# Sigmoid attention and a gated feed-forward product on one core: both dense products by Strassen's algorithm over pairs of batches, and the attention in 64x64 tiles

## The chip, the core and the metric

The kernel runs on one core of a Trainium2 chip. The metric is the device time of one execution in microseconds (us). Of the core's engines, PE (TensorE) multiplies matrices into PSUM, which the program uses as eight banks of 512 fp32 columns on 128 partitions; ACT (ScalarE) and DVE (VectorE) work elementwise and read PSUM as well as the on-chip memory SBUF; POOL (GpSimd) works elementwise and is used here on SBUF alone; SP (SyncE) issues the DMA transfers between DRAM and SBUF. Each engine takes its instructions in the order in which the program issues them to it, and a semaphore holds an instruction until what it needs is there.

## The reference

```python
scores = scale * np.matmul(q, k.transpose(0, 1, 3, 2)) - np.log(S)     # q, k, v: 8 x 12 x 448 x 64
attn = 1.0 / (1.0 + np.exp(-scores))
attn_out = np.matmul(attn, v)
x = attn_out.transpose(0, 2, 1, 3).reshape(B * S, H * D)               # 3584 x 768
h = x @ w_in                                                           # 768 x 2048
g = h * np.clip(h + 3.0, 0.0, 6.0) / 6.0
out = g @ w_out                                                        # 2048 x 768
```

There are 8 batches of 448 tokens and 12 heads of 64 columns. All inputs are float32 and reach the device as they are, the two weight matrices as 64-bit words of two floats each.

## The kernel before, in words

**Products in three passes.** Operands of the two dense products are of type float32r, for which a matmul has one record in the profile. Every such operand is cut in two, a rounded high part and the rest, and each product is high x high, high x rest and rest x high: three matmuls of 128 rows by 128 weight columns by 512 tokens. The first product (`moe_in`, line 240) does, for each of 7 token tiles of 512 and each of 16 blocks of 128 hidden columns, 6 x 3 matmuls into one PSUM bank (L250). ACT then makes relu(h + 3) and DVE multiplies (L254, L255), and the result goes to DRAM. The second product (`moe_out`, line 383) reads it back, splits it, and does 16 x 3 matmuls for each of 7 x 6 blocks of the output (L390). Both products have 2016 matmuls.

**Attention.** Work is in pairs of heads, 64 columns each, so that a pair fills 128 partitions. A head pair has 448 keys, three blocks of 128 and one of 64. A step computes the scores of one block of keys for both heads (L167: each head uses 64 of the rows of the PE array and all 128 columns), ACT makes the sigmoid (L169, 128 x 896), and a later step multiplies with v (L200: 128 rows, 64 columns for each head). The 64-key rests of two head pairs make one step together in four tiles of 64 x 64 (L165, L198). These matmuls are plain fp32, which PE takes in two passes, so that each has two records in the profile (576 for the 288 matmuls of L167). There are 7 steps for two head pairs, 21 for a batch, 168 in all. Scores are issued three steps in a row, then the products with v of the three steps before, and so on. When a head pair is done, ACT copies its rounded part out of PSUM and DVE the rest (L215, L216).

**The two weight matrices.** They come in as 64-bit words. `join_f64` and `split_f32` (lines 46 to 67) take w_in apart on ACT, DVE and POOL in 32 pieces of 128 x 384 while the attention of the first three batches and the first token tile run; DVE's five instructions stand on L51, L52, L53, L56 and L57, POOL's two on L60 and L66. `split_over` (line 69) does the same to w_out on ACT and DVE in 24 pieces of 128 x 512 (L73 to L85), beside the last token tile of `moe_in`. Each weight is prepared once and stays in SBUF.

**The order.** It is written out by hand: attention of batches 0 to 2, `moe_in` of tiles 0 and 1, then attention of one batch and `moe_in` of one tile in turn, and the whole of `moe_out` at the end. POOL has nothing to do after the w_in pieces. SP's order is not part of the hand-written one; a scheduler makes it, in both kernels.

## Time and profile before

| what | value |
|---|---|
| median of three runs | 1212.89 us (1212.23 to 1213.55) |
| profiled execution, first to last instruction | 1209.4 us |
| PE busy | 1200.7 us |
| DVE busy | 365.9 us |
| ACT busy | 372.9 us |
| POOL busy | 64.6 us |
| moved by DMA | 128.84 MB |

The profile is of one execution; its span is 3.5 us below the median of the timed runs. A row of the profile names line, engine, operation, output and inputs, the number of partitions by elements, and then busy time and mean duration of one instruction. "PEld" is the loading of weights into PE, which runs beside the matmuls. The chain of waits follows the last instruction back to what released it; a view in order of time gives start, duration, engine and line.

### The profile page before, as it was taken

How to read it: one execution, taken by the hardware profiler on the slowest of the kernel's cores; microseconds unless marked ns; L12 is line 12 of the kernel's file. 1: busy time of each engine (PE TensorE's matmuls, PEld its weight loads, DVE VectorE, ACT ScalarE, POOL GpSimd, SP SyncE). 2: the span in 40 equal slices, each digit the busy share in tenths (PEclk: the TensorE clock that was granted, in tenths of full speed). 3: DMA queues.
4: the chain of work that ended last, by engine and by line, in shares of the span. 5: the costliest groups of instructions: out<-in, count | busy, mean ns of one | idle time of the engine just before them, and what ended most of it. 6: DMA issues, size and time to landing. Idle time of an engine off the chain costs nothing.

```text
span 1209.4 us, 13744 instructions
## 1 busy us (share of the span) xinstructions
PE 1200.7 (99%) x5568; PEld 852.6 (70%) x5568; DVE 365.9 (30%) x606; ACT 372.9 (31%) x501; POOL 64.6 (5%) x70
## 2 busy tenths in 40 slices
PE   8999999999999999999999999999999999999998
PEld 3334888837855863883785588888888888888887
DVE  3556743111111111111111389871120303030300
ACT  6886321162144135116214444340110202020200
POOL 1334520000000000000000000000000000000000
PEclk9999999999999999999999999999999999999999
DMA  7666421132133114113212278632040404040000
GB/s 241 193 194 184 154 96 62 70 114 76 61 96 95 70 68 122 61 66 115 80 62 80 79 231 292 216 118 109 28 164 27 157 27 165 27 165 18 27 27 27
DMA packets 52433, 128.84 MB, mean 107 GB/s; under 512 B 9233, under 2 KB 16017, under 8 KB 48785
## 3 DMA queue, kind: packets, MB, share of 16 engines
q1 hardware_dynamic: 52080, 127.75, 31.4%
q8 instruction: 44, 0.72, 0.3%
q10 hardware_dynamic: 288, 0.20, 0.1%
q14 instruction: 21, 0.16, 0.0%
HBM read 87.56 MB, written 40.37 MB: 106 GB/s over the span
## 4 chain that ended last, share of the span: by engine, by line
PE 99%; DMA 0%; DVE 0%; ACT 0%; issue 0%
PE ph L250 38%; PE po L390 38%; PE sc L167 10%; PE pv L200 10%; PE sc L165 2%; PE pv L198 2%; DMA qk<-qk 0%; DVE x L216 0%; ACT x L215 0%; DVE o L403 0%; ACT o L406 0%
## 5 line engine op out<-in xcount | busy, mean ns | idle before, releaser
L250 PE MATMUL ph<-x,wi 128*128 128x512 f32 x2016 | 458.9, 389 | 1.3 <-DVE x L216 1.3
L250 PEld LDWEIGHTS ph<-x,wi 128*128 128x128 f32 x2016 | 378.0, 188 | 84.0 <-issue 3.5
L390 PE MATMUL po<-gh,woh 128*128 128x512 f32 x672 | 261.4, 389 | 0.0
L390 PE MATMUL po<-gl,woh 128*128 128x512 f32 x672 | 261.4, 389 | 0.0
L390 PE MATMUL po<-gh,wol 128*128 128x512 f32 x672 | 261.4, 389 | 0.0
L169 ACT ACTIVATE a<-sc,bias_s 128x896 f32<-128x896 f32 x168 | 157.4, 1008 | 51.2 <-PE sc L167 51.0
L254 ACT ACTIVATE g<-ph,bias 128x512 f32<-128x512 f32 x112 | 77.1, 688 | 294.6 <-PE ph L250 288.0
L255 DVE SCALAR_TENSOR_TENSOR g<-g,ph 128x512 f32<-128x512 f32 x112 | 76.9, 686 | 286.8 <-ACT g L254 286.8
L350 ACT CAST gh<-gr 128x2048 fp32r<-128x2048 f32 x28 | 53.6, 1914 | 296.4 <-PE po L390 294.1
L390 PEld LDWEIGHTS po<-gl,woh 128*128 128x128 f32 x672 | 126.1, 188 | 26.4
L390 PEld LDWEIGHTS po<-gh,woh 128*128 128x128 f32 x672 | 126.1, 188 | 26.1
L390 PEld LDWEIGHTS po<-gh,wol 128*128 128x128 f32 x672 | 126.1, 188 | 26.1
L167 PE MATMUL sc<-qk 64*128 64x448 f32 x576 | 127.9, 568 | 3.8 <-DMA qk<-qk 3.8
L200 PE MATMUL pv<-a,v 128*64 128x448 f32 x576 | 122.4, 550 | 0.0
L399 DVE TENSOR_SCALAR o<-po 128x512 f32<-128x512 f32 x41 | 28.3, 690 | 284.0 <-PE po L390 283.9
L167 PEld LDWEIGHTS sc<-qk 64*128 64x128 f32 x576 | 50.6, 189 | 77.3 <-issue 37.1
L200 PEld LDWEIGHTS pv<-a,v 128*64 128x64 f32 x576 | 35.6, 136 | 80.4 <-issue 77.3
L216 DVE TENSOR_TENSOR x<-pv,x 128x448 fp32r<-128x448 f32 (+6 forms) x78 | 32.7, 419 | 194.9 <-ACT x L215 194.9
L351 DVE TENSOR_TENSOR gl<-gr,gh 128x2048 fp32r<-128x2048 f32 x28 | 64.1, 2288 | 30.2 <-ACT gh L350 30.2
L215 ACT CAST x<-pv 128x448 fp32r<-128x448 f32 (+6 forms) x78 | 28.8, 370 | 37.2 <-DVE x L216 14.3
L60 POOL TENSOR_TENSOR wis<-wis 128x384 f32<-128x384 f32 x32 | 32.4, 1011 | 95.3 <-DVE wis L57 95.3
L66 POOL TENSOR_TENSOR wi<-wis,wi 128x384 fp32r<-128x384 f32 x32 | 32.5, 1024 | 7.8 <-ACT wi L65 7.6
(33 smaller groups left out, 307.7 us busy)
## 6 DMA issues: line engine op xcount, KB each, us to landing
gd<-g SPq DMA_DIRECT2D x112, 256.0 KB, 2.4
gr<-gd SPq DMA_DIRECT2D x28, 1024.0 KB, 5.5
qk<-qk SPq DMA_DIRECT2D x47, 448.0 KB, 3.4
wis<-wi SPq DMA_DIRECT2D x32, 384.0 KB, 3.3
ws<-wo SPq DMA_DIRECT2D x24, 512.0 KB, 4.7
outT<-o SPq DMA_DIRECT2D x41, 256.0 KB, 2.0
v<-vP SPq DMA_DIRECT2D x24, 224.0 KB, 2.6
v<-vP SPq DMA_DIRECT2D x24, 192.0 KB, 2.8
```

The costliest lines, as they stand in the source:

```text
L60: nc.gpsimd.tensor_tensor(out=a, in0=a, in1=b, op=ALU.add)
L66: nc.gpsimd.tensor_tensor(out=lo, in0=a, in1=hi.bitcast(F32), op=ALU.subtract)
L167: nc.tensor.matmul(sc[:, j, :S], k[halves[j], c * P : (c + 1) * P], q[halves[j]], start=True, stop=True)
L169: nc.scalar.activation(a, sc[:, :, :S], AF.Sigmoid, bias=bias_s, scale=scale)
L200: nc.tensor.matmul(out, v[:, j * NC + c], a[:, j], start=(p % 2 == 0 and c == 0), stop=(p % 2 == 1 and c == NC - 1),)
L216: nc.vector.tensor_tensor(out=xl, in0=pt[:, q0 : q0 + w], in1=xh.bitcast(F32), op=ALU.subtract)
L250: nc.tensor.matmul(ph, w[:, cc], x, start=(n == 0), stop=(n == 3 * NCC - 1))
L254: i1 = nc.scalar.activation(g, ph, AF.Relu, bias=bias_3, scale=1.0)
L255: i2 = nc.vector.scalar_tensor_tensor(out=g, in0=g, scalar=6.0, in1=ph, op0=ALU.min, op1=ALU.mult)
L350: nc.scalar.copy(gh, gr)
L351: nc.vector.tensor_tensor(out=gl, in0=gr, in1=gh.bitcast(F32), op=ALU.subtract)
L390: nc.tensor.matmul(po[t, ec], w[:, fc], x[:, u], start=(fc == 0 and n == 0), stop=(fc == NFC - 1 and n == 2))
```

## The change

**Strassen.** The tokens of two whole batches (2 x 448) are the two column halves of x; the 768 rows of x and w_in are two halves of 384, the 2048 hidden columns two halves of 1024. The first product is computed with seven products of such quarters in place of eight (in the form with 15 additions), the second likewise with w_out. One matmul now has 448 columns where it had 512, and each of the two products still has 2016 of them: 4 pairs of batches x 8 blocks x 7 products x 9 matmuls. Operands are still cut in two and take three passes.

The sums and differences that the algorithm wants are made in these places. `prep` takes one block of a weight matrix apart (five DVE instructions of 128 x 768, twice), joins it on POOL (four of 128 x 384) and makes the sums of the quarters on POOL (four more); the seven results go to DRAM, for 8 blocks of w_in and 8 of w_out. `t_ops` makes the four differences of x on POOL and cuts the seven operands in two on DVE (`put`: a cast and a subtraction). `quad` does the first product for one block: `split_w1` cuts each weight sum, read back from DRAM for every pair of batches, on ACT and DVE; seven products go to PSUM, three of them onto the bank of the first; ACT keeps two of them, DVE makes c12, h11, h22 and h12 (`add`), ACT and DVE make the gate of each (`gate`), POOL the four differences of g, and seven tiles of 128 x 448 go to DRAM. `block` does the second product with the same cuts (`split_2`), and ACT and DVE form the output.

**Attention in 64 x 64.** Scores and products with v are issued as four matmuls on the four 64 x 64 tiles of the array, for the rests as for the whole blocks. Scores of one step and the product with v of the step two before alternate one by one. Score tiles have two buffers of two banks where there were three, the products with v have four banks, and `take` adds two banks into one tile on ACT and DVE.

**The order.** Every call is put into a list with a place, a time in us that the program works out with 0.82 us for a half step of the attention (TS) and 0.2 us for a matmul of 448 columns (TM); the list is sorted by it and issued. The places set the order on each engine and nothing else. The runs are: batches 0 to 2 and the first product of pair 0; batches 3 and 4 and pair 1; 5 and 6 and pair 2; 7 and pair 3; then the second product. Five of the eight w_in blocks are prepared in the first run of attention, three beside the first quads, and the w_out blocks one every 30 us of place from the first product of pair 1 on, up to that of pair 2.

**What stands on DVE now.** First DVE in the kernel before, in the first product of tile 1, blocks 5 to 10 (g is the gated result, ph the PSUM bank):

```order
L255 SCALAR_TENSOR_TENSOR g_5_1677<-g_5_1677,ph_5_1655 128x512
L255 SCALAR_TENSOR_TENSOR g_6_1700<-g_6_1700,ph_6_1681 128x512
L255 SCALAR_TENSOR_TENSOR g_7_1723<-g_7_1723,ph_7_1704 128x512
L255 SCALAR_TENSOR_TENSOR g_8_1746<-g_8_1746,ph_8_1727 128x512
L255 SCALAR_TENSOR_TENSOR g_9_1769<-g_9_1769,ph_9_1750 128x512
L255 SCALAR_TENSOR_TENSOR g_10_1792<-g_10_1792,ph_10_1773 128x512
```

One instruction stood there for each 18 matmuls of PE. Now DVE in the first product of pair 0, block 1, beside the preparation of w_in block 6 (ab and st are its scratch tiles, w a weight sum and its parts, raw the sum read from DRAM, za and zb PSUM banks, sn the kept sums, ga the gate):

```order
L264 TENSOR_TENSOR w_1_6_1422<-raw_1_1_1216,w_1_6_1422 128x384
L264 TENSOR_TENSOR w_2_0_1438<-raw_2_0_1269,w_2_0_1438 128x384
L301 TENSOR_TENSOR sn_1_c_1456<-za_1_1381,sn_1_1_1436 128x448
L101 TENSOR_SCALAR ab_6_1_1444<-ab_6_1_1444 128x768
L102 TENSOR_SCALAR ab_6_1_1444<-ab_6_1_1444 128x768
L103 SCALAR_TENSOR_TENSOR ab_6_1_1444<-st_6_1_1312,ab_6_1_1444 128x768
L264 TENSOR_TENSOR w_2_1_1461<-raw_2_0_1269,w_2_1_1461 128x384
L111 TENSOR_SCALAR ab_6_1_1444<-ab_6_1_1444 128x768
L112 SCALAR_TENSOR_TENSOR ab_6_1_1444<-st_6_1_1312,ab_6_1_1444 128x768
L301 TENSOR_TENSOR sn_1_h_1479<-zb_1_3_1446,sn_1_0_1420 128x448
L315 SCALAR_TENSOR_TENSOR ga_1_1481<-ga_1_1481,sn_1_h_1479 128x448
L264 TENSOR_TENSOR w_2_2_1484<-raw_2_0_1269,w_2_2_1484 128x384
```

Between the two additions on L301, which read PSUM, stand six instructions that read and write SBUF alone; the gate on L315 stands directly behind the addition that it needs.

**What stands on PE now.** PE in the attention of the kernel before (sc are score tiles, a the sigmoids, pv the banks of the products with v):

```order
L200 MATMUL pv_265<-a_209,v_156 64x448 x2
L200 MATMUL pv_265<-a_214,v_156 64x448 x2
L167 MATMUL sc_286<-qk_185 128x448 x2
L167 MATMUL sc_291<-qk_185 128x448 x2
L167 MATMUL sc_296<-qk_228 128x448 x2
L200 MATMUL pv_265<-a_244,v_156 64x448 x2
L198 MATMUL pv_265<-a_251,v_156 64x448 x2
L198 MATMUL pv_307<-a_251,v_186 64x448 x2
```

And PE in the attention now:

```order
L175 MATMUL sc_1_2_254<-qk_1_130 64x448 x4
L201 MATMUL pv_1_0_264<-a_1_0_237,v_1_131 64x448
L201 MATMUL pv_1_1_265<-a_1_0_237,v_1_131 64x448
L201 MATMUL pv_1_0_264<-a_1_0_237,v_1_131 64x448
L201 MATMUL pv_1_1_265<-a_1_0_237,v_1_131 64x448
L170 MATMUL sc_1_3_276<-qk_1_130 64x448 x2
L170 MATMUL sc_1_3_276<-qk_4_164 64x448 x2
L201 MATMUL pv_1_0_264<-a_1_1_248,v_1_131 64x448
```

Every row has outputs of 64 partitions, and groups of three steps have become groups of one.

The core of the diff, old lines first:

```diff
-                xh, xl = xb[t, cc]
-                for w, x in ((wih[fc], xh), (wih[fc], xl), (wil[fc], xh)):
-                    nc.tensor.matmul(ph, w[:, cc], x, start=(n == 0), stop=(n == 3 * NCC - 1))
-                    n += 1
-                    yield
-            g = xpr.tile([P, T], F32, tag="g", name=f"g_{t}_{fc}", bufs=2)
-            i1 = nc.scalar.activation(g, ph, AF.Relu, bias=bias_3, scale=1.0)
-            i2 = nc.vector.scalar_tensor_tensor(out=g, in0=g, scalar=6.0, in1=ph, op0=ALU.min, op1=ALU.mult)
-            evac.append((i1.ins, i2.ins))
-            nc.sync.dma_start(out=gd[t][fc // GF][:, fc % GF], in_=g)
...
-            for n, (w, x) in enumerate(((woh[ec], gh), (woh[ec], gl), (wol[ec], gh))):
-                nc.tensor.matmul(
-                    po[t, ec], w[:, fc], x[:, u], start=(fc == 0 and n == 0), stop=(fc == NFC - 1 and n == 2)
-                )
...
+            nc.vector.tensor_scalar_min(a, a, F64_TOP)
+            nc.vector.tensor_scalar(out=ai, in0=ai, scalar1=3, scalar2=None, op0=ALU.logical_shift_left)
+            nc.vector.scalar_tensor_tensor(
+                out=ai, in0=high, scalar=-(2**31), in1=ai, op0=ALU.bitwise_and, op1=ALU.bitwise_or
+            )
...
+            nc.vector.tensor_scalar(out=bi, in0=ai, scalar1=-(2**23), scalar2=None, op0=ALU.bitwise_and)
+            nc.vector.scalar_tensor_tensor(
+                out=b, in0=low.bitcast(U32), scalar=2.0**-52, in1=b, op0=ALU.mult, op1=ALU.mult
+            )
...
+                nc.gpsimd.tensor_tensor(out=o, in0=a[:, hs], in1=b[:, hs], op=ALU.add)
...
+            w = wt[0]
+            for o, x, y, op in (
+                (P5, NW, P4, ALU.add), (P6, P5, P1, ALU.subtract), (P7, P1, NW, ALU.subtract), (P3, P2, P6, ALU.subtract)
+            ):
+                nc.gpsimd.tensor_tensor(out=w[:, o], in0=w[:, x], in1=w[:, y], op=op)
...
+        for u in range(2):
+            at(place + u * gap, head, u)
+            at(place + u * gap + 1.0, body, u)
+            at(place + u * gap + 1.5, tail, u)
+        at(place + 2 * gap, sums)
...
-                    nc.tensor.matmul(sc[:, j, :S], k[halves[j], c * P : (c + 1) * P], q[halves[j]], start=True, stop=True)
...
+                for h in range(2):
+                    for j in range(2):
+                        ks = slice(c * P + h * D, c * P + (h + 1) * D)
+                        nc.tensor.matmul(sc[halves[h], j, :S], k[halves[j], ks], q[halves[j]], start=True, stop=True)
...
+                    for h in range(2):
+                        shared = h == (1 - j if second else j)
+                        nc.tensor.matmul(
+                            pv[b, hp][h][halves[j], :S], v[halves[h], j * NC + c], a[halves[h], j],
+                            start=c == 0 and not (second and shared), stop=c == NC - 1 and not (shared and not second),
+                        )
...
+        nc.scalar.copy(x, p0[:, :S])
+        nc.vector.tensor_tensor(out=x, in0=p1[:, :S], in1=x, op=ALU.add)
...
+        nc.vector.tensor_copy(x[:, 0], src)
+        nc.vector.tensor_tensor(out=x[:, 1], in0=src, in1=x[:, 0].bitcast(F32), op=ALU.subtract)
...
+        at(place, diff, P5, raw(b12), raw(b11))
+        at(place + 0.01, place_of, P1, raw(b11))
+        at(place + 1.0, place_of, P2, raw(b21))
+        at(place + 1.1, diff, P6, raw(b22), of(P5))
+        at(place + 2.0, place_of, P5, of(P5))
+        at(place + 2.1, diff, P7, raw(b22), raw(b12))
+        at(place + 3.0, place_of, P3, raw(b22))
+        at(place + 3.1, diff, P4, raw(b21), of(P6))
+        at(place + 4.0, place_of, P6, of(P6))
+        at(place + 5.0, place_of, P7, of(P7))
+        at(place + 6.0, place_of, P4, of(P4))
...
+        nc.scalar.copy(w[:, 0], src)
+        nc.vector.tensor_tensor(out=w[:, 1], in0=src, in1=w[:, 0].bitcast(F32), op=ALU.subtract)
...
+                    nc.tensor.matmul(
+                        z[k][:, :S], w[:, wu, c * P : (c + 1) * P], X[n, k, c][:, xu],
+                        start=i == 0 and k in (P1, P5, P2, P3), stop=i == 3 * HC - 1, skip_group_check=True,
...
+            nc.vector.tensor_tensor(out=t, in0=z[k][:, :S], in1=sn[s], op=ALU.add)
...
+            nc.scalar.activation(g[o], h, AF.Relu, bias=bias_3, scale=1.0)
+            nc.vector.scalar_tensor_tensor(out=g[o], in0=g[o], scalar=6.0, in1=h, op0=ALU.min, op1=ALU.mult)
...
+        def diffs():
+            a, c = g["a"], g["c"]
+            nc.gpsimd.tensor_tensor(out=a[:, 1], in0=g["g12"], in1=g["g11"], op=ALU.subtract)
+            nc.gpsimd.tensor_tensor(out=a[:, 2], in0=g["g22"], in1=a[:, 1], op=ALU.subtract)
...
+        for k in range(NW):
+            at(place + k * TU, product, k)
+            at(place + (k + 1) * TU - 10.0, split_w1, n, j, k)
...
+        at(place + 1 * TU + e, keep, P1)
+        at(place + 2 * TU + e, keep, P5)
+        at(place + 3 * TU + e, add, "c12", P6, P5)
+        at(place + 4 * TU + e, add, "h11", P2, P1)
+        at(place + 4 * TU + e + 0.1, gate, "g11", lambda: sn["h11"])
+        at(place + 5 * TU + e, add, "h22", P7, P5)
+        at(place + 5 * TU + e + 0.1, gate, "g22", lambda: sn["h22"])
+        at(place + 6 * TU + e, add, "h12", P3, "c12")
+        at(place + 6 * TU + e + 0.1, gate, "g12", lambda: sn["h12"])
+        at(place + 6 * TU + e + 0.2, diffs)
+        at(place + 7 * TU + e, gate, "g21", lambda: z[P1][:, :S])
+        at(place + 7 * TU + e + 0.1, last)
...
+        split_w((n, k, u), w2[k][:, u])
...
+        nc.scalar.copy(x[:, 0], src)
+        nc.vector.tensor_tensor(out=x[:, 1], in0=src, in1=x[:, 0].bitcast(F32), op=ALU.subtract)
...
+                for i, (wu, xu) in enumerate(passes):
                     nc.tensor.matmul(
-                        out, v[:, j * NC + c], a[:, j],
-                        start=(p % 2 == 0 and c == 0), stop=(p % 2 == 1 and c == NC - 1),
+                        z[k][e][:, :S], w[:, wu, e * P : (e + 1) * P], x[:, xu],
+                        start=u == 0 and i == 0 and k in (P1, P5, P2, P3), stop=u == HF - 1 and i == 2,
+                        skip_group_check=True,
                     )
...
+    now = 5.0
+    runs = [(0, 1, 2), (3, 4), (5, 6), (7,)]
+    marks = []
+    for n, bs in enumerate(runs):
+        steps = [(b, m, r) for b in bs for m in range(HC) for r in range(LC)]
+        lag = 2
+        for i in range(len(steps) + lag):
+            if i < len(steps):
+                b, m, r = steps[i]
+                at(now, scores, b, m, r)
+                if r in (0, NC):
+                    hp = m + HC * (r == NC)
+                    at(now - 12 if (b, m) != (0, 0) else -20 + r, load_qkv, b, hp)
+                now += TS
+                at(now, sigmoid, b, m, r)
+            if i >= lag:
+                b, m, r = steps[i - lag]
+                at(now, av, b, m, r)
+                now += TS
+                if r in (NC, LC - 1):
+                    hp = m + HC * (r > NC)
+                    at(now + 0.3, take, b, hp)
+                    if b % 2 and r == LC - 1:
+                        t_ops(b // 2, m, now + 1.0)
+        if bs[-1] % 2:
+            now += 8.0
+        marks.append(now)
+        for j in range(HF):
+            quad(n, j, now)
+            now += NW * TU
+    for j in range(HF):
+        prep(0, j, (14 + 20 * j) if j < 5 else marks[0] + 12.6 * (j - 5), 5)
+        prep(1, j, marks[1] + 5 + 30 * j, 9)
```

More of the change, by code (lines that the diff above doesn't have):

```diff
@@ L187, in av @@
[L187 to L199 removed]
+                    h = j if u == 0 else 1 - j
@@ new lines, in tile_kernel, with order @@
+    for j in range(HF):
+        prep(0, j, (14 + 20 * j) if j < 5 else marks[0] + 12.6 * (j - 5), 5)
+        prep(1, j, marks[1] + 5 + 30 * j, 9)
+    att_end = marks[3] + 8
+    at(att_end, open_two)
+    at(now + 3.0, close_one)
+    first = now
+    for n in range(NT):
+        block(n, now)
+        now += NW * HF * TU
+    def order(item):
+        place, i, f, args = item
+        if f is load_w2 and args[0] >= 2:
+            place = max(place, first + 3.01)
+        return place, i
+    todo.sort(key=order)
@@ L409, in tile_kernel @@
[L409 to L414 removed]
+        for _, _, f, args in todo:
+            f(*args)
 def kernel(q, k, v, moe_w_in, moe_w_out):
```

564 lines of the change are left out of this document (257 added, 307 removed).

## The prediction

> **What bounds the kernel now.** The head of the page comes first, then the chain of waits in order of time.
>
> ```profile
> PE 1200.7 (99%) x5568; PEld 852.6 (70%) x5568; DVE 365.9 (30%) x606; ACT 372.9 (31%) x501; POOL 64.6 (5%) x70
> ```
>
> ```profile
> 0.73 3.07 DMA qk<-qk
> 3.85 4.49 PE sc L167 x12
> ...
> 21.29 2.40 PE pv L200 x12
> 23.69 2.46 PE sc L167 x12
> ...
> 112.02 130.82 PE ph L250 x576
> 242.84 2.52 PE sc L167 x12
> ...
> 278.25 65.53 PE ph L250 x288
> ...
> 748.93 456.97 PE po L390 x2016
> ```
>
> PE is busy from 3.85 us to the end and the chain stays on it, so today time is the number of matmuls times their spacing. In the first product that is 130.82/576 = 227.1 ns, in the second 456.97/2016 = 226.7 ns, for 512 columns. One batch of attention takes from 242.84 to 278.25 = 35.4 us, 21 steps. Everything else is hidden, and the list of waits gives PE one wait of any size inside the run:
>
> ```profile
> PE ph L250 <- DVE x L216: 1.3, 1, 1.3
> ```
>
> The question is therefore how much shorter PE's work becomes, and whether DVE and POOL, which get far more to do, can still hide.
>
> **The matmuls of the two products.** Their number stays 2016 each; columns go from 512 to 448. In proportion a matmul would take 198.3 ns; if nothing in it shrank, 226.7. I take 200.0, near the proportion with a small fixed part: 4032 x 0.2000 = 806.4 us in place of 457.9 + 457.0 = 914.8, that is -108.4 us (-115 to 0).
>
> **The attention.** The loads of PE's weights show the matmuls' beat, since each pair of loads goes with a pair of matmuls:
>
> ```profile
> 47.12 0.14 PEld L200 LDWEIGHTS pv<-a,v 128*64 128x64 f32 x2 [0.23 <-issue]
> 47.50 0.14 PEld L200 LDWEIGHTS pv<-a,v 128*64 128x64 f32 x2 [0.23 <-issue]
> 47.88 0.14 PEld L200 LDWEIGHTS pv<-a,v 128*64 128x64 f32 x2 [0.23 <-issue]
> ...
> 51.18 0.21 PEld L198 LDWEIGHTS pv<-a,v 64*64 64x64 f32 x8 [0.65 <-issue]
> 52.09 0.20 PEld L200 LDWEIGHTS pv<-a,v 128*64 128x64 f32 x4 [0.70 <-issue]
> ```
>
> Inside one tile shape a pass comes every 0.38 us, so a half step (two passes) takes 0.76. Four 64 x 64 tiles do the same work at once, but alone between other shapes they took 52.09 - 51.18 = 0.91: leaving a shape cost 0.15. Now all are 64 x 64 and no shape is left inside a run: 336 half steps x 0.76 = 255.4 us against 8 x 35.4 = 283.3, -27.9 us. The ends are 0.82 each (2.46/3, -7.8) and 0.91, if each half step still drained (+22). With two score buffers, PE waits some 0.4 us for the first sigmoid of each of four runs: +2.
>
> **What DVE, ACT and POOL must do.** Groups by line give mean durations, DVE's first, then ACT's, then POOL's:
>
> ```profile
> L53 DVE SCALAR_TENSOR_TENSOR wis<-wis 128x384 int32<-128x384 int32 x32 | 19.3, 602 | 1.1
> L57 DVE SCALAR_TENSOR_TENSOR wis<-wis 128x384 f32<-128x384 uint32 x32 | 17.9, 558 | 1.1
> L76 DVE SCALAR_TENSOR_TENSOR wa<-ws,wa 128x512 int32<-128x512 int32 x24 | 16.4, 684 | 0.1
> L51 DVE TENSOR_SCALAR wis<-wis 128x384 f32<-128x384 f32 x32 | 15.3, 480 | 17.3 <-ACT wis L50 16.9 <-issue 0.4
> L52 DVE TENSOR_SCALAR wis<-wis 128x384 int32<-128x384 int32 x32 | 14.3, 447 | 1.1
> L56 DVE TENSOR_SCALAR wis<-wis 128x384 int32<-128x384 int32 x32 | 11.5, 360 | 1.1
> L74 DVE TENSOR_SCALAR wa<-wa 128x512 f32<-128x512 f32 x24 | 10.1, 422 | 11.3 <-ACT wa L73 11.2
> L216 DVE TENSOR_TENSOR x<-pv,x 128x448 fp32r<-128x448 f32 x12 | 7.5, 625 | 46.5 <-ACT x L215 46.5
> L184 DVE CAST x<-pend 128x320 fp32r<-128x320 f32 x6 | 1.9, 320 | 0.0
> ```
>
> ```profile
> L50 ACT ACTIVATE wis<-wis 128x384 f32<-128x384 f32 x32 | 17.9, 560 | 0.1
> L65 ACT CAST wi<-wis 128x384 fp32r<-128x384 f32 x32 | 16.5, 515 | 25.1 <-POOL wis L60 25.1
> L73 ACT ACTIVATE wa<-ws 128x512 f32<-128x512 f32 x24 | 16.3, 678 | 50.4 <-DMA ws<-wo 40.5 <-DVE wol L85 4.7 <-DVE g L255 2.8
> L215 ACT CAST x<-pv 128x448 fp32r<-128x448 f32 x12 | 6.4, 534 | 5.5 <-PE pv L200 3.0 <-PE pv L198 2.4
> ```
>
> ```profile
> L60 POOL TENSOR_TENSOR wis<-wis 128x384 f32<-128x384 f32 x32 | 32.4, 1011 | 95.3 <-DVE wis L57 95.3
> ```
>
> Scaled to their new widths: two tensors of 384 elements 0.56, of 448 0.62, of 768 0.94 (0.56 + 3 x 0.126); one tensor with scalars of 768 0.55; the cast of 448 0.38; an addition from PSUM 0.625; POOL 1.01 and, for 448, 1.18. A quad (7 products, 12.6 us of PE) then asks DVE for 7 x 0.56 + 4 x 0.625 + 4 x 0.62 = 8.9 us. Three of its gates stand directly behind the addition whose relu ACT must first make (0.62 plus the hand-over, 0.7), so DVE waits 2.1 more: 11.0. A `prep` costs DVE 2 x (3 x 0.55 + 2 x 0.94) = 7.06 and POOL 8 instructions; a quad gives POOL 4. ACT has 7 x 0.515 + 2 x 0.534 + 4 x 0.62 = 7.2 of 12.6 and stays behind DVE. In the second product a unit of 1.8 us asks ACT for about 1.1 and DVE for 1.2, split eight units ahead, and POOL is idle: hidden.
>
> **DVE beside POOL.** DVE in order of time, then POOL, at a place where both work:
>
> ```profile
> 115.59 1.05 DVE L52 TENSOR_SCALAR wis<-wis 128x384 int32<-128x384 int32 x1
> 116.68 1.26 DVE L53 SCALAR_TENSOR_TENSOR wis<-wis 128x384 int32<-128x384 int32 x1
> 117.97 0.36 DVE L56 TENSOR_SCALAR wis<-wis 128x384 int32<-128x384 int32 x1
> ```
>
> ```profile
> 115.37 1.06 POOL L60 TENSOR_TENSOR wis<-wis 128x384 f32<-128x384 f32 x1 [5.44 <-DVE wis L57]
> 116.39 1.13 POOL L66 TENSOR_TENSOR wi<-wis,wi 128x384 fp32r<-128x384 f32 x1
> ```
>
> A DVE instruction that meets a POOL one takes 0.70 us longer (1.05 against 0.36, 1.26 against 0.56) and ends 0.2 to 0.4 after it: they don't share, one waits. How often they met is in the means: L51, L52 and L53 lie 0.12, 0.09 and 0.04 over the undisturbed 0.36 and 0.56, 0.25 us for two POOL instructions, 0.125 each or 18% of the 0.70, with DVE about half busy. Beside a nearly full DVE they meet more often; I take the middle between 0.125 and meeting two times in three (0.47).
>
> [...]
>
> **What that adds to PE's time.** PE depends on DVE closely in a quad: the addition after product P6 must be done before P7, one product (1.8 us) later, and that of P7 before P4.
> - 23 quads without `prep`: 11.0 + 4 x 0.125 = 11.5 at best, 13.4 with three meetings of 0.8, against 12.6: +0.3 each, 7 us (0 to 18).
> - 3 quads of pair 0 with a w_in `prep` each: 11.0 + 7.06 + 12 x 0.125 = 19.6 to 23.9 (8 meetings of 0.72): +7.0 to +11.3 each; 27 us (21 to 34).
> - Of the eight w_out `prep`s, 18 us long and 30 apart by their places, 5.5 fall into quads: 7.06 + 1.0 to 3.8, less 1.6 of spare time: +6.5 to +9.2 each; I take 7.5, 41 us (36 to 51).
> - Attention of batch 1: three blocks of 7 x 1.52 = 32 us bring DVE 21 `put`s of 1.0, two `prep`s and 6 x 0.625 = 38.9 us, and POOL 28 instructions (3.5 to 13 us of DVE's time). `take` stands behind them on DVE, and PE needs its banks again after about 3 us: +12 (7 to 17). Batch 5, with one `prep` in its last two blocks: +4 (1 to 7). Batches 3 and 7 fit.
> - Before the last quads PE waits for `take`, `put` and POOL's differences of the last heads: P1's part is there 0.53 + 0.625 + 1.0 = 2.2 us after the attention, P6's at 6.2 to 9.8 where two products cover 3.6; 1.3 of it is there today: +4 (2 to 9).
>
> **Transfers.** Bytes go from 129 to about 249 MB.
>
> ```profile
> 683.00:749.00 66.00, 65.65 (x290) 54.36 (x291) 57.34 (x107) 28.56 (x44) 0.00 (x0) 1.00 0.74 247
> ```
>
> In this stretch (the last columns are clock, DMA share and GB/s) 247 GB/s took 0.74 of the DMA engines, so 334 would fill them. A quad moves 2.98 MB (237 GB/s), with a w_out `prep` 335 in all, and a quad with a w_in `prep` 5.9 MB, 17.8 us. I cost that at nothing, since DVE needs 20 us or more there; without that cover it would be 3 x 5 us. On SP a load of the next raw weights waits for the last split and holds stores of g behind it, whose tiles are free for 12.6 us. The end, a scaling and a store, stays as it is.
>
> **The sum.** 1209.4 - 108.4 - 27.9 + 2 + 4 + 91 = 1170.1 us of span. The median stands 3.5 above the profiled span: 1173.6 us. Its own range is 1135 to 1207.
>
> **The rivals.**
> - [...] POOL meets DVE wherever it can and PE's pauses cost clock. The waits come to their upper ends: 18 + 34 + 51 + 17 + 7 + 2 + 9 = 138. After an idle start the first 12 score matmuls took 4.49 where the same later took 2.46, 2.0 us more; some 17 long pauses in quads with a `prep` would add 34. 1209.4 - 136.3 + 172 + 3.5 = 1248.6. It decides from 136 us of waits on. For it speaks how strictly the two serialise; against it, that they met only in 18% so far. [...]
> - *All fits, fast.* DVE's waits for ACT fall into time that it had spare, and meetings stay at 18%: 3 x 4.9 (8.9 + 7.06 + 1.5 - 12.6), 5.5 x 2.8 (8.1 less 3.7 of spare time in 1.43 quads), 8 in the attention and 4 at starts make 42. 1209.4 - 136.3 + 42 + 3.5 = 1118.6. DVE's own sum, 8.9 of 12.6, speaks for it; the gates directly behind their additions speak against.
> - *The narrower matmul is not shorter.* A load of weights takes most of a matmul's spacing:
>
> ```profile
> L250 PEld LDWEIGHTS ph<-x,wi 128*128 128x128 f32 x2016 | 378.0, 188 | 84.0 <-issue 3.5
> ```
>
> 188 ns of 227, and it doesn't shrink with the columns. If it sets the beat, the 108 us are not gained and some 25 of DVE's waits hide in the longer quads: 1173.6 + 108.4 - 25 = 1257. Against it: loads idle 84 us between matmuls.
>
> **How the numbers follow.** Runs of this kernel differ by about 0.1%, so 0.2% (1210.5 to 1215.3) is what can be told from no change. Chances: forecast 0.45, fast 0.25, slow 0.24, not shorter 0.06. The forecast is faster in 0.42 of its 0.45, the same in 0.02; the slow case is the same in 0.01. Faster 0.67, same 0.03, slower 0.30. The range runs from 1100, the fast case with matmuls of 198.3 ns and no wait left for the last heads, to 1250, where the slow case lies.
>
> **What would show it.** Right: matmuls of both products every 200 ns; half steps of 0.76; the second product at 403 us without a gap; PE idle behind DVE's L301 and L210, most in the first three quads and near every `prep`; DVE rows of L264 and L315 with means well over 0.56 and 0.62. Wrong: 227 ns at 448 columns; 0.9 a half step; PE waiting for DMA or ACT in quads; waits under 60 or over 136 us in all.

## The result, and the profile after

The kernel after takes **1306.47 us** (median of four runs, 1302.4 to 1309.08) against 1212.56 for the kernel before beside it: a ratio of 1.077, with a 95% interval of 1.0751 to 1.0794. It is slower, and 57 us slower than the slower end of the range.

The page's head and two of its slices; the slices cut the span of 1306.2 us into 40 parts.

```profile
PE 1153.3 (88%) x6720; PEld 904.8 (69%) x6720; DVE 878.1 (67%) x1352; ACT 649.4 (50%) x1150; POOL 376.2 (29%) x310
...
PE   8877767899987889788689968989999999999998
...
PEclk9978887999988888898899989999999999999999
```

PE was 99% busy before and is 88% busy now, and its granted clock, in tenths, falls below 9 in most of the slices in which it pauses. Next the view by stretches, cut where PE passes from attention to the first product and back. The columns are the length, then busy time and number of instructions of PE, PEld, DVE, ACT and POOL, then the granted clock, the DMA share and GB/s.

```profile
3.80:135.60 131.80, 107.11 (x1009) 48.02 (x1009) 85.14 (x114) 79.44 (x96) 54.74 (x49) 0.91 0.62 224
135.60:285.90 150.30, 117.07 (x509) 102.90 (x505) 108.62 (x145) 53.21 (x105) 69.11 (x56) 0.90 0.66 228
285.90:351.00 65.10, 64.37 (x673) 28.15 (x672) 39.01 (x60) 49.72 (x60) 19.65 (x16) 1.00 0.45 140
351.00:496.00 145.00, 118.01 (x512) 104.28 (x508) 110.99 (x151) 55.42 (x106) 67.99 (x54) 0.89 0.69 228
496.00:578.10 82.10, 70.79 (x673) 30.18 (x672) 61.38 (x82) 52.77 (x64) 37.89 (x32) 0.92 0.57 184
578.10:716.90 138.80, 114.83 (x510) 102.27 (x506) 96.82 (x138) 52.39 (x103) 62.99 (x50) 0.90 0.64 212
716.90:749.55 32.65, 31.96 (x338) 12.63 (x337) 20.01 (x30) 24.50 (x29) 14.56 (x12) 1.00 0.26 86
749.55:885.20 135.65, 112.31 (x508) 97.94 (x505) 96.35 (x146) 53.78 (x110) 43.20 (x32) 0.95 0.58 207
885.20:1302.00 416.80, 416.80 (x2017) 378.37 (x2016) 259.83 (x492) 225.80 (x477) 5.71 (x4) 1.00 0.43 162
```

Two stretches of attention run as they should: batches 3 and 4 take 65.1 us, batch 7 takes 32.65, at full clock. Batches 0 to 2 take 131.8 where three times 32.6 is 97.8, and batches 5 and 6 take 82.1. The first product takes 150.3 + 145.0 + 138.8 + 135.65 = 569.7 us; the forecast gave it 403.2 and 79 of waits. The second has no gap and takes 416.8 instead of 403.2. The attention's four stretches make 311.7 us; before's 286.5, less 27.9, with the forecast's 18 us of waits would be 276.6. By stage the 136 us between forecast and trace are thus 87 in the first product, 35 in the attention and 14 in the second product.

PE's largest waits (total, times, longest), and then DVE and POOL in order of time in a quad of pair 0:

```profile
PE za L288 <- DVE sn_c L301: 48.4, 13, 6.7
PE za L288 <- DVE sn_h L301: 47.6, 21, 5.3
PE pv L201 <- DVE xr L210: 23.5, 4, 7.1
```

```profile
166.14 1.50 DVE L101 TENSOR_SCALAR ab<-ab 128x768 f32<-128x768 f32 x1
167.68 1.39 DVE L102 TENSOR_SCALAR ab<-ab 128x768 int32<-128x768 int32 x1
169.11 0.96 DVE L103 SCALAR_TENSOR_TENSOR ab<-st,ab 128x768 int32<-128x768 int32 x1
170.10 0.56 DVE L111 TENSOR_SCALAR ab<-ab 128x768 int32<-128x768 int32 x1
...
173.31 0.61 DVE L301 TENSOR_TENSOR sn_c<-za,sn 128x448 f32<-128x448 f32 x1
```

```profile
165.76 1.47 POOL L321 TENSOR_TENSOR gc<-gc,g 128x448 f32<-128x448 f32 x1
167.19 1.46 POOL L329 TENSOR_TENSOR gt<-g,ga 128x448 f32<-128x448 f32 x1
171.73 2.51 POOL L118 TENSOR_TENSOR wt<-ab 128x384 f32<-128x384 f32 x2 [3.08 <-DVE ab L112]
```

L101 and L102 take 1.50 and 1.39 beside POOL, and L111, of the same size, 0.56 without it. The addition c12 at 173.31 stands behind all of them, and PE waits for it. What PE pays then is in PE's own rows:

```profile
173.97 3.61 PE L288 MATMUL za<-x,w 128*128 128x448 f32 x9 [4.92 <-DVE sn_c L301]
177.42 1.99 PE L288 MATMUL zb<-x,w 128*128 128x448 f32 x9
```

The pause is 4.92 us, and the nine matmuls behind it take 3.61 where the next nine take 1.99; the granted clock is 0.51 from 173.97 to 177.40 us and 1.00 in the two us behind that. Over the whole first product pauses make 113.7 us and slow matmuls some 40.

One thing was not in the forecast in any form. These are POOL, SP and ACT in a quad of pair 3, with no preparation near:

```profile
828.24 1.35 POOL L319 TENSOR_TENSOR ga<-g,ga 128x448 f32<-128x448 f32 x1 [8.86 <-DVE g L315]
...
832.40 1.47 POOL L329 TENSOR_TENSOR gt<-g,ga 128x448 f32<-128x448 f32 x1
```

```profile
831.46 0.32 SPq L257 DMA_DIRECT2D raw<-wd  x1
831.87 0.38 SPq L323 DMA_DIRECT2D gd<-ga  x1
```

```profile
836.63 0.67 ACT L314 ACTIVATE ga<-sn_h,bias 128x448 f32<-128x448 f32 x1 [4.85 <-DMA gd<-ga]
```

ACT's next gate writes the tile `ga`, of which there is one. It waits 4.85 us until the last of three stores from it has landed, and that store was issued behind POOL's work and behind a load of raw weights. ACT's queue, with the splits in it, stands meanwhile, and such quads take 14.5 us each instead of 13.0.

### The profile page after: what moved, and what is told of

The parts are those of the page before. It is cut to its first block, busy times and chain, and to the rows that moved or that the text cites. A ratio compares the mean times of both kernels' runs of the same rounds, so it can differ in the third digit from the quotient of the medians.

```text
span 1306.2 us, 18625 instructions
## 1 busy us (share of the span) xinstructions
PE 1153.3 (88%) x6720; PEld 904.8 (69%) x6720; DVE 878.1 (67%) x1352; ACT 649.4 (50%) x1150; POOL 376.2 (29%) x310
## 5 line engine op out<-in xcount | busy, mean ns | idle before, releaser
L288 PE MATMUL za<-x,w 128*128 128x448 f32 x1152 | 291.6, 407 | 106.2 <-DVE sn_c L301 48.4
L288 PEld LDWEIGHTS za<-x,w 128*128 128x128 f32 x1152 | 240.1, 212 | 146.7 <-issue 57.6
L397 PE MATMUL y<-x,w 128*128 128x448 f32 x1344 | 314.0, 368 | 0.0
L397 PEld LDWEIGHTS y<-x,w 128*128 128x128 f32 x1344 | 252.4, 188 | 25.4
L264 DVE TENSOR_TENSOR w<-raw,w 128x384 fp32r<-128x384 f32 x224 | 185.2, 837 | 43.8 <-ACT w L263 41.7
L288 PE MATMUL zb<-x,w 128*128 128x448 f32 x864 | 196.2, 372 | 1.3 <-DVE x L217 1.1
L201 PE MATMUL pv<-a,v 64*64 64x448 f32 x1152 | 168.8, 561 | 28.1 <-DVE xr L210 23.5
L288 PEld LDWEIGHTS zb<-x,w 128*128 128x128 f32 x864 | 167.1, 194 | 17.3 <-DVE x L217 1.5
L397 PE MATMUL yb<-x,w 128*128 128x448 f32 x672 | 175.1, 368 | 0.0
L175 PE MATMUL sc<-qk 64*64 64x448 f32 x1152 | 160.7, 554 | 13.1 <-ACT a L181 7.7
L314 ACT ACTIVATE ga<-sn_h,bias 128x448 f32<-128x448 f32 x32 | 21.4, 669 | 155.2 <-DMA gd<-ga 70.2
```

What stands on the lines that cost most here:

```text
L175: nc.tensor.matmul(sc[halves[h], j, :S], k[halves[j], ks], q[halves[j]], start=True, stop=True)
L201: nc.tensor.matmul(pv[b, hp][h][halves[j], :S], v[halves[h], j * NC + c], a[halves[h], j], start=c == 0 and not (second and shared), stop= ...
L264: nc.vector.tensor_tensor(out=w[:, 1], in0=src, in1=w[:, 0].bitcast(F32), op=ALU.subtract)
L288: nc.tensor.matmul(z[k][:, :S], w[:, wu, c * P : (c + 1) * P], X[n, k, c][:, xu], start=i == 0 and k in (P1, P5, P2, P3), stop=i == 3 * HC ...
L314: nc.scalar.activation(g[o], h, AF.Relu, bias=bias_3, scale=1.0)
L397: nc.tensor.matmul(z[k][e][:, :S], w[:, wu, e * P : (e + 1) * P], x[:, xu], start=u == 0 and i == 0 and k in (P1, P5, P2, P3), stop=u == H ...
```

## The experiments

Two theories were set against each other at first. **A:** PE waits because DVE is full, its work lengthened where it meets POOL's, as in the 1.50 and 1.39 us above; the expectations call that POOL's lock. **B:** PE waits in loops through single buffers and stores. **C**, a smaller one: SP starts the second product's first loads too early. Later runs split A: DVE's own work, its place in the order, the lock, the slow clock.

The stage times of all runs, in us, each from PE's first matmul of a stage to the first of the next (the second product's to its last). Stages and span are those of the profiled execution, the time is the median of all executions:

| run | attention | first product | second product | span | time |
|---|---|---|---|---|---|
| before | 286.5 | 458.4 | 457.1 | 1209.4 | 1212.6 |
| after | 311.7 | 569.7 | 416.6 | 1306.2 | 1306.5 |
| e1 gates apart | 312.2 | 546.3 | 408.6 | 1275.5 | 1277.7 |
| e2 no preparation | 373.8 | 477.7 | 408.6 | 1268.1 | 1273.5 |
| e3 POOL narrow | 269.6 | 537.0 | 416.6 | 1231.3 | 1233.2 |
| e4 SP planned | 326.2 | 614.2 | 408.6 | 1357.7 | 1359.7 |
| e5 narrow pass | 312.7 | 570.9 | 366.8 | 1258.4 | 1260.2 |
| e6 gate late | 314.0 | 559.9 | 408.7 | 1291.2 | 1291.6 |
| e7 spread | 337.7 | 501.7 | 408.6 | 1256.4 | 1262.9 |
| e8 all | 337.1 | 518.6 | 416.4 | 1280.3 | 1282.9 |
| e9 spread apart | 303.6 | 500.3 | 408.6 | 1220.6 | 1230.6 |
| e10, the same again | 305.6 | 499.8 | 416.6 | 1230.1 | 1232.2 |
| e11 sums on DVE | 294.4 | 512.6 | 416.6 | 1231.8 | 1229.6 |
| e12 two a | 281.8 | 508.9 | 416.6 | 1215.9 | 1219.0 |
| e13 in window | 291.5 | 514.7 | 416.6 | 1231.4 | 1226.8 |
| e14 filler | 315.0 | 564.1 | 416.6 | 1304.0 | 1302.2 |
| e15 POOL 8 | 269.2 | 429.2 | 408.6 | 1115.4 | 1118.5 |
| e16 preparation's DVE 8 | 280.7 | 457.5 | 408.6 | 1155.0 | 1156.4 |

### e1: gates and differences in tiles of their own

```diff
-                g["a"] = one.tile([P, 3, S], F32, tag="ga", name=f"ga_{n}_{j}")
-                g[o] = g["a"][:, 0]
+            g[o] = one.tile([P, S], F32, tag=o, name=f"{o}_{n}_{j}")
...
-            nc.gpsimd.tensor_tensor(out=a[:, 1], in0=g["g12"], in1=g["g11"], op=ALU.subtract)
+            nc.gpsimd.tensor_tensor(out=g["d5"], in0=g["g12"], in1=g["g11"], op=ALU.subtract)
```

> Each gate and each of POOL's differences in a tile of its own, instead of one tile of three (ga) and one of two (gc); the same work, the same room. Theory B (in a quad without preparation the next gate waits until all three stores of the single ga tile have landed, and those wait for POOL's four operations and for a load of raw weights ahead of them on SP): the five last quads of pair 3 go from 14.5 to 13.0-13.3 us, other quads without preparation likewise, and the whole from 1306 to 1265-1290. Theory A (what makes PE wait is the amount of DVE's work, lengthened where POOL meets it): those quads keep 14.0-14.6 and the whole changes by under 8 us.

PE's waits in five of pair 3's quads of the kernel after (797 to 870 us) were this one row; e1 has none in the same five.

```profile
PE za L288 <- DVE sn_h L301: 7.1, 5, 1.6
```

Those quads went from 14.3-14.6 to 12.8-13.0 us, the first product from 569.7 to 546.3. B holds for the quads without a preparation. Those with one (24.6, 26.5, 26.0 us in pair 0) did not move. Of the 28.8 us gained 8 are the second product's, which is told at the end.

### e2: no arithmetic in the preparation

```diff
-                nc.gpsimd.tensor_tensor(out=w[:, o], in0=w[:, x], in1=w[:, y], op=op)
+                pass
...
-            at(place + u * gap, head, u)
-            at(place + u * gap + 1.0, body, u)
-            at(place + u * gap + 1.5, tail, u)
+            pass
```

> Leaves out the arithmetic of the weight preparation on ACT, DVE and POOL; its loads and stores stay (what is stored is a constant tile). Theory A: the quads that have a preparation beside them (16.5 to 26.7 us) fall to the 14.5 of those without, the first product goes from 570 to about 480, the attention of batches 0 to 2 from 132 to about 112; 1306 becomes 1185-1210. Theory B alone (loops through stores, loads and single buffers): under 40 us gained, 1265-1306, since those transfers remain.

The quads with a preparation fell to 12.9-15.9 us, and pairs 0 to 2 lost 92 us, as A has it. The total, 1273.5, did not follow and lies in B's range, for a reason of the experiment's own: with nothing to wait for, SP issued the stores and loads of the preparations at once, and the attention of batches 0 to 2 took 210.9 us behind them (PE waited 50.7 us for q and k, the longest 30.0). Only the quads can be read here.

### e3: POOL's work in preparations and head pairs over 8 columns

```diff
-                nc.gpsimd.tensor_tensor(out=o, in0=a[:, hs], in1=b[:, hs], op=ALU.add)
+                nc.gpsimd.tensor_tensor(out=o[:, :8], in0=a[:, hs][:, :8], in1=b[:, hs][:, :8], op=ALU.add)
```

> POOL's eight additions of each preparation and its four differences for each head pair are made over 8 columns instead of 384 and 448 (the rest of those tiles is a constant); all instructions and waits stay in their places, only POOL is done at once and hardly ever beside DVE; POOL's four operations in each quad stay whole. If it is the meeting of DVE and POOL (about 0.49 us of DVE for each of 176 POOL operations, 86 us) that makes the waits: 1306 becomes 1225-1260, and the means of DVE's rows in the preparation fall to 0.56 and 0.96. If it is the amount of DVE's work by itself: 1285-1306, quads of pair 0 with a preparation stay over 22 us. Theory B: no change outside the preparation.

73 us were gained, with the same instructions in the same order: batches 0 to 2 went from 131.8 to 104.6, batches 5 and 6 from 82.2 to 67.9, the three w_in quads from 24.6, 26.7 and 25.8 to 19.2, 21.2 and 21.3. DVE's busy time fell with it, from 878.1 to 798.3 us, 0.45 for each of the 176 POOL operations. So POOL's work is most of the price in the attention, and 5 us of each such quad's 12. One expectation missed: the means of the preparation's DVE rows fell little (L101's from 812 to 750 ns); POOL's four whole operations in each quad were still there to meet.

### e4 and e8: SP's order, and the second product's first operands

e4 only adds SP to the engines whose order is planned. e8 adds to e6 and e7, below, that four transfers are issued by ACT:

```diff
-        nc.sync.dma_start(out=t, in_=wd2[k])
+        (nc.scalar if k < 2 else nc.sync).dma_start(out=t, in_=wd2[k])
```

> SP's DMA issues also in the planner's order, nothing else. Theory C (SP starts the 6.7 MB of the second product's first operands in the first quad of pair 3 and they hold up the raw weights): the first two quads of pair 3 go from 27.7 and 20.3 to 20-22 and 14.5, 10 to 15 us in all, 1290-1297. Theory A: those two are long because DVE does the last heads' parts: no change over 5 us. Loads that now stand behind stores that wait could also come later: then slower by up to 20.

> Gates in tiles of their own, their DVE half late, the preparations spread, and the first operands of the second product (6.7 MB) started from ACT's queue at their planned place, 26 us before that product, instead of by SP in the first quad of pair 3. Theory A with B and C: the first two quads of pair 3 go from 27 and 22 to 18-20 and 13.5; the whole 1140-1205, below the kernel before. If the lock decides: 1235-1270.

e4 was 53 us slower, though the first two quads of pair 3 came down from 27.7 and 20.3 to 25.1 and 17.2. ACT's wait for the stores of `ga` rose from 70.2 to 113.1 us:

```profile
ACT ga L314 <- DMA gd<-ga: 113.1, 17, 11.9
```

e8 shows C on its own spot. In the kernel after, SP's rows in the first quad of pair 3 were these (gr and w are the second product's operands):

```profile
763.86 0.33 SPq L371 DMA_DIRECT2D gr<-gd  x1
764.24 0.42 SPq L366 DMA_DIRECT2D w<-wd  x1
...
775.48 14.82 DMA raw<-wd
```

The last row is from the chain of waits: the next raw weights landed 14.82 us after their issue. In e8 the second quad of pair 3 took 13.0 us; it took 20.3 in the kernel after and 21.3 in e7. The first quad stayed at 27.8: it waits for DVE's parts of the last heads. So C is worth 8 us. As a whole e8, at 1282.9, lies above both of its ranges. It contains e6, and its quads without a preparation are at 14.3 us again.

### e5: every third matmul of the second product narrower

```diff
+            wide = (S, 384, 320, 256, 192, 128, 64)[k]
...
+                    s = S if i < 2 else wide
```

> In the second product every third matmul (the third pass over each pair of tiles) covers 448, 384, 320, 256, 192, 128 or 64 columns, for the seven products in their order; the rest stays (those columns of the third pass are left out). If the columns set the beat: each 64 columns fewer shorten that matmul by 20 to 27 ns, down to some 60 ns at 64, and the second product takes about 350 us. If the load of weights (188 ns, with 15 to 19 ns between two of them) sets it: every matmul keeps 203-207 ns whatever its columns, and the product keeps 408 to 417 us.

By shape, with the mean duration of one:

```profile
L399 PE MATMUL y<-x,w 128*128 128x448 f32 x960 | 260.7, 376 | 0.2 <-DVE x L379 0.2
...
L399 PE MATMUL y<-x,w 128*128 128x384 f32 x64 | 21.6, 338 | 0.0
L399 PE MATMUL y<-x,w 128*128 128x320 f32 x64 | 19.8, 309 | 0.0
L399 PE MATMUL y<-x,w 128*128 128x256 f32 x64 | 17.8, 279 | 0.0
...
L399 PE MATMUL y<-x,w 128*128 128x64 f32 x64 | 12.3, 192 | 0.0
```

From 384 columns down every 64 columns are worth 29 ns, down to 64 columns. The distance from start to start follows (203, 175, 147, 114 ns at 448, 384, 320, 256), until the mean over three matmuls reaches 173 ns at 256 columns; from there to 64 it only falls to 171, since the matmul behind the narrow one comes later. Something that does not depend on the columns sets the beat there, and not at 448. The loads of weights are the likely cause, but this run does not show it. The rival of the load falls.

### e6: DVE's half of a gate later

```diff
+        at(place + 4 * TU + e + late, mult, "g11", lambda: sn["h11"])
```

> On top of the gates in tiles of their own (1277.7): the DVE half of three gates in each quad stands 1 us of plan later than its relu, so that DVE makes a split in between instead of waiting 0.74 us for ACT. If DVE's time decides in quads with a preparation, 2 us less in each of some 16: 1240-1262. If what decides is the latency of the chain from a product through its addition to the next product, nothing is gained: 1270-1285.

14 us slower than e1: the quads without a preparation were back at 14.3, those with one unchanged. The delay won back nothing of DVE's 0.74 us of waiting at each gate; why it lengthens the other quads isn't settled.

### e7, e9, e10, e11, e12: the preparations elsewhere

```diff
-        prep(0, j, (14 + 20 * j) if j < 5 else marks[0] + 12.6 * (j - 5), 5)
-        prep(1, j, marks[1] + 5 + 30 * j, 9)
+        prep(0, j, *w_in[j])
+        prep(1, j, *w_out[j])
```

> On top of the gates in tiles of their own (1277.7): the preparations stand elsewhere, six of w_in and four of w_out in those batches of attention whose heads DVE has not to split (0, 2, 4, 6), the other six beside quads but with their ten DVE operations 2.4 to 3 us apart. The same work in all. If what counts is that DVE is overfull where a preparation meets quads or splits (theory A): attention of batches 0 to 2 goes from 132.7 to 102-112, of 5 and 6 from 82 to 66-72, quads from 546 to 480-510, the whole to 1175-1225. If POOL's lock on DVE takes its price wherever it stands: the waits only move, 1250-1285.

The first product fell to 501.7 and the attention rose to 337.7; the whole, 1262.9, lies in the second range. PE's waits there were for sigmoids, and ACT's row says why: its first step of a preparation waits for POOL on the single tile `ab`, with the sigmoids behind it in the queue.

```profile
ACT ab L95 <- POOL wt L121: 45.1, 9, 9.3
```

> The spread preparations (1262.9) again, but 18 to 20 us of plan apart and with 9 us between their halves, so that ACT's first step of a half need not wait for POOL's last addition of the half before (single tile ab) and hold up the sigmoids behind it; the first operands of the second product started from ACT; and the splits of the first quad of pairs 0 and 3 ahead of the last heads' parts on DVE. If the 33 + 8 us that PE waited for sigmoids in batches 0 to 2 came from that: attention of batches 0 to 2 from 149 to 105-115, runs 1 and 2 from 78 to 66-70, the first two quads of pair 3 from 27 and 21 to 18-20 and 13; the whole 1262.9 to 1175-1205, under the kernel before. If DVE with POOL's lock is simply full (716 us of work for 677 us of PE): the waits move elsewhere, 1225-1250.

Farther apart, the attention came down to 303.6 and the first two quads of pair 3 to 23.6 and 12.8; the whole to 1230.6 (ratio to before 1.0143, 1.0102 to 1.0185), over the expected 1175-1205 and in the range given for a full DVE. e10 is a second execution of this same kernel; its label belongs to the next one:

> A second look at the kernel of the run before, for the spread of its stages from run to run: each stage within 2 us, but the second product either 408.6 or 416.6 us.

The stages agreed within 2 us, and the second product took 416.6 where e9 had 408.6.

> As e9, with the eight additions of each preparation on DVE instead of POOL. If a met POOL operation costs DVE what it would cost itself (0.49 against 0.55 for 384 columns), the time stays within 10 us of e9, and what the chain through POOL cost comes back as a small gain. If POOL's operations are mostly free for DVE: slower by 128 x 0.55, up to 70 us.

1229.6, the same as e9 within 1 us, though both kernels vary by 11 us or more between executions. DVE's own time did not stay the same. Its busy time rose from 866.1 to 908.1 us, by 42.0, and the 128 additions take 83.4 us on it (means of 604 and 779 ns). So on POOL they had cost DVE about 41 us, 0.32 each, half of what they cost on DVE. By stage the attention won 9 us and the first product lost 12.

> As e9, with two buffers for the tile that ACT writes first in each half of a preparation (the ring of split weights gives one of its eight for the room), so that ACT's in-order queue with its sigmoids need not stop for POOL; w_out's preparations in the attention start after the last split of the heads before; and in the last batch the second head pair's parts stand behind the take of the last heads on DVE. If PE's waits in the attention are ACT's queue held by that buffer: runs 1 and 2 from 73 and 74 to 66-68, batches 0 to 2 from 123 to 110-118; first quad of pair 3 from 23.6 to 16-19; the whole 1230.6 to 1198-1215, level with the kernel before or under it. If DVE is full, the waits move to DVE's rows: 1220-1240.

With two buffers for ACT's tile the row above is gone, and runs 1 and 2 of the attention take 66.1 and 66.5 us. The first quad of pair 3 stayed at 23.4, where 16 to 19 was expected. The whole came to 1219.0, 1.0043 of the kernel before (1.0027 to 1.0058), between its two ranges. In this kernel the load for one half of w_out's second block in each run is issued before the first block's half has been read, so a part of w_out is wrong; the amount of work is the same.

### e13: preparation only between two additions; e14: pauses filled

```diff
+    def beside(n, k):
+        return marks[n] + k * TQ + after_h22, TQ, 1.3
```

> As e12, but each preparation beside quads has its DVE operations only between the addition of P7 (h22) and the next quad's addition of P6 (c12), five in one quad and five in the next, so that none stands in front of the two additions that PE waits for; two of w_in and six of w_out stand so, six of w_in and two of w_out in the attention; and in pair 3 ACT makes the casts of the last two head pairs' parts. If PE's waits come from the order on DVE (an addition has 1.86 us until PE needs it, 1.24 without its own time): the six or seven quads of each pair that have a preparation go from 16-20 to 13-15 us, the first product from 509 to 455-475, the whole from 1219 to 1170-1190. If they come from the amount of DVE's work with POOL's lock: the waits only move, the first product keeps 495-515, the whole 1205-1225.

The quads with a preparation stayed at 17 to 20 us and the first product at 514.7; the whole, 1226.8, is just above the second range. Nearly all of the wait in the quads is now at c12, the first addition behind the window:

```profile
PE za L296 <- DVE sn_c L309: 57.6, 21, 4.2
```

Each preparation costs PE some 10 us beside quads wherever its instructions stand. Not the place decides: DVE is nearly full there, busy for 83 to 95% of each of these quads. Where it isn't, a preparation costs nothing: runs 1 and 2 of the attention, with one each, took 64.9.

```diff
+                for _ in range(12):
+                    nc.tensor.matmul(z[P3][:, :S], z["w"][:, 0, :P], X[n, P2, 0][:, 0], start=True, stop=True)
```

> The kernel after with 12 extra matmuls ahead of product P7 in 18 quads that have a preparation beside them or start pair 3; they need nothing and their results are overwritten. They fill 2.5 us of a pause of 2.3 to 7. If the slow clock after each pause over 2 us costs the time that the trace shows (39 us in the first product): pauses under 2 us keep the full clock, and the first product goes from 570 to 545-560. If the slow products only use time that DVE needs to catch up anyway: it keeps 565-575. If the fillers themselves cost: over 580.

The slow matmuls fell from 41 to 24 us and the pauses from 113.7 to 82.5, with 216 x 0.207 = 45 us of fillers in their place: the first product lost 5.6 us, at the border of the second case. In 12 of the 18 quads the pause of 2.3 to 6.9 us stood where the fillers went; the slow matmuls of these fell by 8 us, and they took 254.2 us in all where they had taken 254.1. The slow time that the fillers took away there was thus time in which PE would have waited for DVE in any case. In the other six quads no pause stood at that place, so they don't test this.

### e15 and e16: POOL's time away, or the preparation's DVE time

e15 makes every one of POOL's 304 operations over 8 columns in e13's kernel, e16 the preparation's ten DVE operations:

```diff
-            nc.gpsimd.tensor_tensor(out=g["d5"], in0=g["g12"], in1=g["g11"], op=ALU.subtract)
+            nc.gpsimd.tensor_tensor(out=g["d5"][:, :8], in0=g["g12"][:, :8], in1=g["g11"][:, :8], op=ALU.subtract)
```

```diff
-            low, high = st[u][:, :, 0], st[u][:, :, 1]
-            a, b = ab[u]
+            low, high = st[u][:, :8, 0], st[u][:, :8, 1]
+            a, b = (x[:, :8] for x in ab[u])
```

> The kernel of e13 with every operation of POOL (in preparations, head pairs and quads) over 8 columns instead of 384 or 448; DVE, ACT and PE do all their work. If POOL's lock on DVE (about 0.55 us for each of some 300 operations, 165 us of DVE) is what the waits are made of: quads with a preparation go from 17-20 to 13.0-14.5, the first product from 515 to 430-455, the whole from 1226.8 to 1115-1150, well below the kernel before. If DVE's own work is enough to fill it: quads with a preparation keep 16-18, the whole 1170-1205.

> The kernel of e13 with DVE's ten operations of each preparation over 8 columns instead of 768 (7.06 us of DVE's work each, 113 in all, are gone; what the preparation then makes is no weight); POOL does all its work. If it is DVE's sum of work that counts, wherever it comes from: as in e15, quads with a preparation 13-14.5, the whole 1120-1160. If only POOL's lock counts: quads with a preparation keep 16-18, the whole over 1180.

e15 takes **1118.5 us** (ratio to before 0.9227, 0.92 to 0.9254). The heads of e13's and e15's pages and the row of PE's longest wait in e15:

```profile
PE 1133.5 (92%) x6720; PEld 890.8 (72%) x6720; DVE 892.8 (73%) x1338; ACT 659.2 (54%) x1164; POOL 395.4 (32%) x310
```

```profile
PE 1084.7 (97%) x6720; PEld 861.0 (77%) x6720; DVE 728.7 (65%) x1338; ACT 657.9 (59%) x1164; POOL 101.8 (9%) x319
...
PEclk9999999999999999999999999999999999999999
```

```profile
PE za L306 <- DVE sn_c L319: 9.8, 10, 2.0
```

DVE does the same 1338 instructions in both and is busy 892.8 - 728.7 = 164 us less: 0.54 us for each POOL operation. The rows of one group show it, the splits of w beside POOL in e13 and in e15:

```profile
L272 DVE TENSOR_TENSOR w<-raw,w 128x384 fp32r<-128x384 f32 x224 | 191.6, 866 | 23.3 <-ACT w L271 22.2
```

```profile
L282 DVE TENSOR_TENSOR w<-raw,w 128x384 fp32r<-128x384 f32 x224 | 123.3, 553 | 49.2 <-ACT w L281 48.5
```

866 ns against 553; the kernel after has 837. In e16 DVE is busy for 791.5 us, 101 less than in e13, and 70 us are gained (1156.4); its quads with a preparation take 14.0 to 15.6. Attention and first product together, which leaves out the second product's own 8 us, won 107.8 us in e15 for 164 us of DVE's time and 68.0 in e16 for 101: 0.66 and 0.67 us for each us of DVE, whichever engine's work was taken away. So it is DVE's sum that decides, and POOL's operations are a larger part of it than the width of the preparation's. With POOL's operations this short, e13's form of the change is faster than the kernel before by 94 us.

## Why the prediction was wrong

- **Matmuls of the products: nearly right.** 206.7 ns (202.7 in other executions) in place of 200.0: 13.5 us more in each product than the forecast had. The second product gained 40 us where 54 were forecast.
- **Attention in 64 x 64: right.** 65.1 us for batches 3 and 4 are 84 half steps of 0.775; the forecast said 0.76.
- **The step that failed: the price of a meeting and the waits from it.** The prediction read from two rows that DVE's instruction waits for POOL's, 0.70 us each time, and then took "the middle between 0.125 and meeting two times in three (0.47)", that is 0.30 for each POOL operation. It was 0.45 for POOL's work in preparations and head pairs of the kernel after (e3) and 0.54 for all of it in e13 (e15), three quarters of the 0.70: by this estimate most POOL operations meet a DVE instruction where DVE is nearly full. For the preparation's additions alone it was 0.32 in e9 (e11). With 0.54 the prediction's own sum for a quad with a w_in preparation, 11.0 + 7.06 + 12 x 0.54, is 24.5 us, and these quads took 24.6, 26.7 and 25.8. At this price the waits are no longer near 91 us: the first product alone has 113.7 of pauses, the attention of batches 0 to 2 lost 34 and that of 5 and 6 lost 17 where 12 and 4 were forecast. Quads with a w_in preparation lost 11.6 to 13.7 each against 13.0, not 9.
- **"stores of g ... whose tiles are free for 12.6 us": false.** They are not free: three stores share one tile with the next gate. It is in no term of the sum and costs 23 us in the first product (e1).
- **"I cost that at nothing": nearly.** The DMA engines were busy for 0.69 of a stage at most, but 6.7 MB issued early held the raw weights back once, 8 us (e8).
- **The slow clock** was left out of the sum and priced at 2.0 us a pause in the slow rival. The trace has 25 pauses of over 1.9 us in the first product and about 1.6 us of slow matmuls behind each; but in the 12 quads where e14 tests it, taking 8 us of it away gained nothing.

The case that came is the slow rival, at 1248.6. Its mechanism, DVE's work lengthened beside POOL's, is shown by e15 (164 us of DVE's time); what it lacked are the matmuls (27), the single tile (23) and the early transfers (8). That these with it make 1307 is luck: by stage, with the three added, it has 594 us for the first product and 285 for the attention, where 570 and 312 were measured. Against the forecast the three make 58 of the 136 us. Of the other 78, 304 x 0.24 = 73 us more of DVE's time make some 48 at the 0.66 of e15, an estimate; what the remaining 30 are is open. The chance of 0.24 for it was too low, since its own evidence, how strictly the two serialise, weighed more than a share of meetings taken from a kernel whose DVE was half idle.

Not every DVE instruction is longer beside POOL. The splits of w, which read two tensors from SBUF, are (866 ns in e13 against 553 in e15), and so is L101, which reads one (1.50 us at 166.14 beside POOL, 0.56 at 175.21 without). The additions on L301, which read one input from PSUM and one from SBUF, are not: in the kernel after their means are 614 to 617 ns in all four groups, none of the 128 takes over 626, and the one at 157.53 takes 0.61 us while POOL works from 157.27 to 160.80.

No version here with all of its work beats the kernel before. The nearest, e12's, is 0.4% slower and has a part of w_out wrong; of those that compute everything the nearest are e13's and e11's, 1.2% slower. Whether the work that POOL adds could go elsewhere than to POOL or DVE was not tried.

## What to carry to other kernels

Work that was given to POOL to relieve DVE relieved it here by less than it seems: each POOL operation of 384 or 448 columns cost DVE 0.32 to 0.54 us (e11, e3, e15), where one of 384 takes 0.55 on DVE itself (e15). Compare DVE's whole sum with PE's time stage by stage before trusting that such work hides. A share of collisions measured on a half idle engine says little about a full one: 18% of the 0.70 us became three quarters. And before calling a buffer free, list who still reads it: here a tile with three stores from it was free only when the last had landed, 4.85 us into ACT's wait, with all that stood before that store in its queue.

## What was not expected of the hardware

- **Two beats of the same matmuls.** With nothing waiting, the 2016 matmuls of the second product take 416.6 us in some executions and 408.6 in others. In the first, every one starts 206 or 207 ns after the last; in the second the distances go through 199, 202, 203 and 207. The same kernel did both (e9 and e10). What chooses isn't known; 8 us of every comparison here can be this.
- **A short pause can be enough for the slow clock.** A pause is counted here from start to start, less 207 ns. After 23 of the 25 pauses of over 1.9 us in the kernel after's first product the next matmuls came every 373 ns; after the 14 pauses of 0.82 to 1.77 us none did. The granted clock was 0.51 behind the pause of 4.92 us above. No sharp limit shows: in e14 only 10 of 16 pauses of over 1.9 us were followed so, and one of 3.1 us was not. The shortest pause of the 23 was 1.91 us, and five more were of 2.27 to 2.85.
- **A floor under narrower matmuls.** With a new load of 128 x 128 weights for each, matmuls started every 171 to 173 ns on the mean and no faster, however narrow every third one was (e5), though the row of the same loads in the kernel after says 188.
